# Decay attention and a mixture of experts: weights loaded a chunk later, ranks corrected by a small product, one fill instead of two, splits 6 pieces ahead

## The chip, the cores and the metric

The kernel runs on one core of one Trainium2 chip. The metric is the device time of one execution in microseconds, as the median of repeated runs. TensorE is called PE below, VectorE DVE, ScalarE ACT, GpSimd POOL, and SyncE SP; SP only issues transfers here.

## The reference, cut to what matters

Attention with a decay, in blocks, over 2 batches, 8 heads, 768 positions and head size 64; its output, as 1536 tokens of 512 numbers, goes into a mixture of 8 experts. Each token goes to the expert with the largest logit, at the next free place there; an expert takes at most 384 tokens.

```
intra = (qb @ kb.T * Dmask) @ vb
inter = (qb * lam_pow) @ kv_state
out[block] = intra + inter
kv_state = lam_block * kv_state + (kb * rev_pow).T @ vb
...
logits = x @ w_gate;  expert_idx = argmax(logits);  gate_w = softmax(logits)[expert_idx]
for i in range(N):                       # places in the order of the tokens
    e = expert_idx[i]
    if counts[e] < capacity: disp[e, counts[e]] = x[i]; counts[e] += 1
h = relu(disp @ w1);  y = h @ w2;  out[i] = gate_w[i] * y[expert_idx[i], pos[i]]
```

## The kernel before

The program is written out in one order by hand; each engine runs its own instructions in that order, and waits where data or a buffer is missing. It has three stages.

**Attention, 12 chunks of 128 positions** (the loop `for s in range(NTILE)`; two batches of 6 chunks). Step `s` places chunk `s-2`, multiplies chunk `s` with its masked scores (`attend`, line 442, and 450 for the part from the state), adds to the state (`state`, line 476, then `stt` on DVE, line 484), turns the output of chunk `s-1` into rows of tokens and logits (`turn`, lines 493 and 495), and makes the scores of chunk `s+2` (`score`, line 422). `choose` finds the expert of each token on DVE and ends with the one-hot rows `oh` (line 516). `place` multiplies `oh` with a triangle of ones and the running counts `cum` with ones, so that `rank` is the token's row in the DRAM table `xs`; `scatter` writes the rows there by an indirect transfer from POOL. POOL also makes `kd` and `qd`, the decayed keys and queries of later chunks.

**Weights.** They come as 64 pieces of 512 KB, 8 for each expert. `load_w` issues a piece on SP into one of 4 buffers `wraw`; `split_hi` on ACT makes its rounded part `whi`, and `split_lo` on DVE the rest `wlo` (line 113). The tables LOAD, HI and LO say in which step of the attention a piece is loaded and split: before, piece 0 is loaded in step 1, split on ACT in step 3 and on DVE in step 4. Since ACT and DVE take their work in order, a piece that is late holds what stands behind its split.

**Expert 0 early, then 7 experts.** Expert 0 gets its first 128 tokens from the first 7 chunks (EARLY) as the class `Solo`: `up`, `cross` (a transpose of the hidden rows), `down`; `first` runs between the end of the attention and the others, `second` holds a second 128 tokens. `shift()`, in step 8, counts the tokens of expert 0 in the first 7 chunks (a product into `early`, line 554) and adds what is missing to 128 into the running counts (line 559), so that later tokens of expert 0 begin at row 128. After the last chunk `count()` counts all tokens and makes `padi`, the row numbers of unused places, to which `pad` writes zeros by indirect transfers; `fill()` writes zeros over the whole place of FILLED experts at the start, and these need no `pad`. `load_rows(e)` reads an expert's rows back; it is on SP, so weight loads issued after it wait behind it. For the experts 1 to 7, `shuffle` and `trans` turn the rows (DVE, ACT, DVE), then come four products `h` (lines 778 and 782), each with `hf`, `hh`, `hl` on ACT and DVE, then four products `y` (line 810). After each of these eight, `next_w(j)` splits piece `j + 10` and loads piece `j + 14`.

Of the kernel before, what the change touches and what calls it, by code (L numbers as in the profile page):

```python
# [10 lines left out]
F16 = mybir.dt.float16  # L11
# [24 lines left out]
FILLED = 2  # L36
XO = 188
LOAD = {1: (0,), 2: (1,), 3: (2,), 4: (3, 4), **{s: (s,) for s in range(5, 12)}}
HI = {s: s - 3 for s in range(3, 12)}
LO = {s: s - 4 for s in range(4, 12)}  # L40
# [3 lines left out]
def kernel(  # L44
# [44 lines left out]
    padi = const.tile([P, E, 2], I32, name="padi")  # L89

# [10 lines left out]
    def split_hi(i):  # L101
        if i >= E * NWP:
            return
        hi = wsp_p.tile([P, WP], F32R, tag="whi", name="whi")
        nc.scalar.activation(out=hi, in_=raw[i], func=AF.Copy)  # L105
        wsp[i] = (hi, None)
# [144 lines left out]
    def attention():  # L251
        with ExitStack() as c2:
# [70 lines left out]
            nc.gpsimd.memset(zero, 0.0)  # L323
# [21 lines left out]
            def fill():  # L345
                for e in range(FILLED):
                    nc.sync.dma_start(
                        out=xs[e * STR:e * STR + RS].rearrange("(t p) c -> p t c", p=P),
                        in_=zero[:, None, :].to_broadcast([P, 2, ROW]),
                    )  # L350

            def tokens():
                nc.gpsimd.tensor_scalar(
                    out=base8, in0=iota_i, scalar1=float(STR), scalar2=None, op0=ALU.mult
                )
                nc.gpsimd.iota(padi, pattern=[[STR, E], [P, 2]], base=0, channel_multiplier=1)
                nc.gpsimd.tensor_copy(row, padi)
                nc.gpsimd.iota(toki, pattern=[[P, NTILE]], base=0, channel_multiplier=1)
                nc.gpsimd.tensor_copy(tokf, toki)
                nc.gpsimd.tensor_scalar(  # L360
                    out=xg_all[:, :, DM + 1], in0=tokf, scalar1=-1.0,
                    scalar2=float(NT), op0=ALU.mult, op1=ALU.add,
                )
# [121 lines left out]

            def turn(s):

                if s < 0:
                    return
                t = ps_1.tile([P, 2 * DM], F32, tag="tp", name="tp")  # L490
                tp[s] = t[:, 0:KD * XO].rearrange("p (k c) -> p k c", c=XO)
                nr[s] = t[:, 2 * DM - E:2 * DM]
                nc.tensor.matmul(nr[s], lhsT=ones, rhs=num, start=True, stop=True)
                for k in range(KD):
                    nc.tensor.matmul(tp[s][:, k, 0:P + E], lhsT=xT[s][:, k], rhs=iw[:, k], start=True, stop=True)  # L495

# [39 lines left out]
            def place(s):  # L536
                if s < 0:
                    return
                nc.tensor.matmul(rank, lhsT=upper, rhs=oneh[s], start=True, stop=False)
                nc.tensor.matmul(rank, lhsT=ones, rhs=cum[s], start=False, stop=True)  # L540
# [10 lines left out]
            def shift():  # L551

                c = cum[EARLY]
                nc.tensor.matmul(early, lhsT=ones, rhs=c, start=True, stop=True)
                nc.vector.tensor_scalar(
                    out=short, in0=early[:, 0:1], scalar1=float(P), scalar2=-1.0, op0=ALU.min, op1=ALU.mult
                )
                nc.vector.tensor_scalar(out=short, in0=short, scalar1=float(P), scalar2=None, op0=ALU.add)
                nc.vector.tensor_tensor(out=c[0:1, 0:1], in0=c[0:1, 0:1], in1=short[0:1], op=ALU.add)
# [26 lines left out]
            for s in range(NTILE):  # L586
# [14 lines left out]
                if s == EARLY + 1:  # L601
                    shift()
# [3 lines left out]
                choose(s - 1)  # L606
                rows(s - 1)
# [10 lines left out]
                load(s + 6, 0)  # L618
                if s == EARLY + 1:
                    load_rows(0, 0)  # L620
# [20 lines left out]
            def count():  # L641
                nc.tensor.matmul(early, lhsT=ones, rhs=cum[NTILE], start=True, stop=True)
# [13 lines left out]
            first.up(2, (tail(2), None, None))  # L656
            load_rows(0, 1)
            load_rows(1)
            first.cross(0)
            first.up(3, (count, None, None))  # L660
            split_lo(8)
            split_hi(9)
            first.down(0)
            first.cross(1)
            load_w(12)
            split_lo(9)
            load_w(13)
# [3 lines left out]
    def ffn(first):  # L671
        with ExitStack() as c2:
# [33 lines left out]
            def next_w(j):  # L706
                split_w(j + 10)
                load_w(j + 14)
# [26 lines left out]
            second.up(0)  # L735
            split_lo(10)
            load_w(14)
            second.up(1)
            split_hi(11)
            split_lo(11)  # L740
            load_w(15)
            second.up(2)
            shuffle(1, 0)
            second.cross(0)
            trans(1, 0)
            split_hi(12)
            second.up(3)
            split_lo(12)
            load_w(16)
            shuffle(1, 1)  # L750
            second.down(0)
            second.cross(1)
            trans(1, 1)
            for i, p in ((13, 1), (14, 2), (15, 3)):
                split_w(i)
                load_w(i + 4)
                second.down(p)
            pad(3, 0)
            pad(3, 1)
            split_w(16)  # L760
            load_w(20)
            split_w(17)
            load_w(21)
# [274 lines left out]
```

## Time and profile before

| | us |
|---|---|
| median of 3 runs | 260.01 |
| fastest and slowest of them | 259.89, 261.07 |
| the profiled execution, its own time | 257.97 |
| its span, first to last instruction | 256.2 |
| PE busy in the span | 237.2 (93%) |
| DVE busy | 172.2 (67%) |
| ACT busy | 144.6 (56%) |
| POOL busy | 76.9 (30%) |

Busy time of PE is modelled from pipelined starts, so it does not say how near PE is to its peak. The profiled execution lies 2.0 us under the median of the runs; 1.8 us of its own time lie outside the span.

### The profile page before, as it was taken

The page shows a single profiled execution, that of the slowest core. Times are in us where ns is not written, and L with a number is a line of the kernel's source. Part 1 is how long each engine was busy: PE and PEld are TensorE (multiplying, and loading weights), DVE is VectorE, ACT ScalarE, POOL GpSimd, SP SyncE. Part 2 cuts the span into 40 slices and gives each one's busy share as a digit, 9 for nine tenths or more (in the row PEclk, how much of TensorE's full clock was granted, in tenths as well). Part 3 has the DMA queues.
Part 4 walks back from the last instruction along what each step waited for, and adds up shares of the span by engine and source line. Part 5 has one row for each costly group of instructions (what it writes and reads, how often), then busy time and mean ns, then how long its engine had stood idle before and what let it go on. Part 6 is the DMA issues. An engine that isn't in the chain of part 4 may idle for free.

```text
span 256.2 us, 4967 instructions
## 1 busy us (share of the span) xinstructions
PE 237.2 (93%) x1832; PEld 199.7 (78%) x1832; DVE 172.2 (67%) x323; ACT 144.6 (56%) x267; POOL 76.9 (30%) x100
## 2 busy tenths in 40 slices
PE   7897998769799988899999999999999999999991
PEld 3686887658698967777987797798798789779891
DVE  5654677897536587669677777966976896683400
ACT  2225556938643585666656756765685576653310
POOL 7565557657230711000700330070051021011031
PEclk9999999999999999999999999999999999999998
DMA  5999999985537767965859859786884989602011
GB/s 121 410 338 377 411 387 406 412 313 178 174 147 172 257 180 242 303 222 194 262 137 324 244 179 288 260 260 157 280 274 158 294 242 273 186 0 75 0 42 26
DMA packets 27246, 58.94 MB, mean 230 GB/s; under 512 B 6274, under 2 KB 13444, under 8 KB 27216
## 3 DMA queue, kind: packets, MB, share of 16 engines
q1 hardware_dynamic: 23296, 51.41, 63.0%
q0 software_dynamic: 3216, 7.14, 7.4%
q8 instruction: 16, 0.26, 0.5%
q14 instruction: 14, 0.11, 0.2%
q10 hardware_dynamic: 704, 0.02, 0.2%
HBM read 50.37 MB, written 11.22 MB: 240 GB/s over the span
## 4 chain that ended last, share of the span: by engine, by line
issue 32%; PE 26%; DMA 15%; DVE 11%; ACT 6%; POOL 5%; SPq 2%; POOLq 1%; DVEq 0%; ACTq 0%
PE y L810 9%; DMA qk<-in_qkv 8%; PE h L778 7%; DMA wraw<-in_wp 6%; DVE wlo L113 4%; PE h L782 3%; ACT whi L105 3%; POOL xs L132 2%; PE tp L495 2%; POOL out L181 2%; PE x L442 2%; DMA xs<-zero,padi 2%; DVE hf L788 1%; PE sc L422 1%; ACT hh L791 1%
## 5 line engine op out<-in xcount | busy, mean ns | idle before, releaser
L113 DVE TENSOR_TENSOR wlo<-wraw,whi 128x1024 fp32r<-128x1024 f32 x64 | 78.2, 1233 | 14.0 <-ACT whi L105 12.6
L778 PE MATMUL h<-xhl,whi 128*128 128x464 f32 x224 | 73.6, 381 | 2.1 <-DVE hf L788 1.3
L105 ACT ACTIVATE whi<-wraw 128x1024 fp32r<-128x1024 f32 x64 | 66.0, 1046 | 14.2 <-DMA wraw<-in_wp 14.2
L782 PE MATMUL h<-xhl,wlo 128*128 128x232 f32 x224 | 60.2, 269 | 0.0
L181 POOL DMA_INDIRECT out<-y,ti x13 | 15.3, 1179 | 117.8 <-ACT y L819 116.0
L778 PEld LDWEIGHTS h<-xhl,whi 128*128 128x128 f32 x224 | 42.0, 188 | 9.1 <-DVE hf L788 1.9
L782 PEld LDWEIGHTS h<-xhl,wlo 128*128 128x128 f32 x224 | 42.7, 190 | 0.3
L810 PE MATMUL y<-whi,hh 128*128 128x512 f32 (+1 forms) x104 | 41.1, 396 | 0.0
L810 PE MATMUL y<-whi,hl 128*128 128x512 f32 (+1 forms) x104 | 41.1, 395 | 0.0
L810 PE MATMUL y<-wlo,hh 128*128 128x512 f32 (+1 forms) x104 | 40.9, 393 | 0.0
L791 ACT ACTIVATE hh<-hf 128x464 fp32r<-128x464 f32 x28 | 16.6, 592 | 32.4 <-DVE hf L788 32.4
L792 DVE SCALAR_TENSOR_TENSOR hl<-hf,hh 128x464 fp32r<-128x464 f32 x28 | 18.0, 643 | 18.4 <-ACT hh L791 18.4
L788 DVE TENSOR_TENSOR hf<-h,hf 128x464 f32<-128x464 f32 x28 | 17.8, 636 | 8.0 <-ACT hf L787 8.0
L810 PEld LDWEIGHTS y<-whi,hl 128*128 128x128 f32 (+1 forms) x104 | 18.6, 179 | 5.7
L810 PEld LDWEIGHTS y<-wlo,hh 128*128 128x128 f32 (+1 forms) x104 | 18.6, 179 | 5.4
L810 PEld LDWEIGHTS y<-whi,hh 128*128 128x128 f32 (+1 forms) x104 | 18.6, 178 | 5.3
L430 DVE TENSOR_TENSOR pt<-sc,dt 128x512 f32<-128x512 f32 x24 | 16.2, 687 | 4.1 <-PE sc L422 3.8
L787 ACT ACTIVATE hf<-h 128x464 f32<-128x464 f32 x28 | 15.3, 545 | 5.9 <-PE h L782 5.9
L565 POOL DMA_INDIRECT xs<-xg,slot x12 | 12.3, 1025 | 20.7 <-ACT slot L564 16.5
L422 PE MATMUL sc<-qk 64*128 64x128 f32 x192 | 14.2, 285 | 2.6 <-DMA qk<-in_qkv 2.6
L422 PEld LDWEIGHTS sc<-qk 64*128 64x128 f32 x192 | 11.9, 187 | 4.5 <-DMA qk<-in_qkv 2.7
L500 ACT ACTIVATE xg<-tp 128x512 f32<-128x512 f32 x12 | 7.1, 590 | 13.3 <-DVE oh L516 13.3
(127 smaller groups left out, 339.6 us busy)
## 6 DMA issues: line engine op xcount, KB each, us to landing
wraw<-in_wp SPq DMA_DIRECT2D x64, 512.0 KB, 5.0
qk<-in_qkv SPq DMA_DIRECT2D x12, 512.0 KB, 10.9
kv<-in_qkv SPq DMA_DIRECT2D x12, 512.0 KB, 11.2
rw<-xs SPq DMA_DIRECT2D x28, 128.0 KB, 3.1
xs<-zero SPq DMA_DIRECT2D x2, 514.0 KB, 10.8
rw<-xs SPq DMA_DIRECT2D x2, 257.0 KB, 3.7
out<-y,ti POOLq DMA_INDIRECT x13, 6.1
xs<-xg,slot POOLq DMA_INDIRECT x12, 5.2
```

The lines of the kernel that those rows point to most:

```text
L105: nc.scalar.activation(out=hi, in_=raw[i], func=AF.Copy)
L113: nc.vector.tensor_tensor(out=lo, in0=t, in1=hi.bitcast(F32), op=ALU.subtract)
L181: i = nc.gpsimd.indirect_dma_start(out=out, out_offset=bass.IndirectOffsetOnAxis(ap=ti[e][0:m, t:t + 1], axis=0), in_=y[0:m], in_offset=No ...
L422: nc.tensor.matmul(sc[s][r][:, a], lhsT=kT[rs, a], rhs=qT[rs, a], start=True, stop=True)
L430: nc.vector.tensor_tensor(out=pt[s][:, r], in0=sc[s][r], in1=dt[:, r], op=ALU.mult)
L778: nc.tensor.matmul(ps[:, f, 0:2 * SLOT], lhsT=wh[:, k, fs], rhs=x2[:, k], start=(k == 0), stop=False, skip_group_check=True,)
L782: nc.tensor.matmul(ps[:, f, 0:SLOT], lhsT=wl[:, k, fs], rhs=x2[:, k, 0], start=False, stop=(k == KD - 1), skip_group_check=True,)
L787: nc.scalar.activation(out=hf, in_=ps[:, :, SLOT:2 * SLOT], func=AF.Copy)
L788: nc.vector.tensor_tensor(out=hf, in0=ps[:, :, 0:SLOT], in1=hf, op=ALU.add)
L791: nc.scalar.activation(out=hh, in_=hf, func=AF.Relu)
L792: nc.vector.scalar_tensor_tensor(out=hl, in0=hf, scalar=0.0, in1=hh.bitcast(F32), op0=ALU.max, op1=ALU.subtract)
L810: nc.tensor.matmul(yp[t][0:m], lhsT=a[:, f, tsl], rhs=b[:, f], start=(p == 0 and f == 0 and n == 0), stop=(p == 3 and f == 1 and n == 2),)
```

## The change

It has six parts.

1. LOAD, HI and LO stand one step later for the first pieces: piece 0 is loaded in step 2, split on ACT in step 4, on DVE in step 5; pieces 9 and 10 are loaded together in step 11. Before step 12 eleven pieces are loaded instead of twelve, eight split on ACT instead of nine, seven on DVE instead of eight.
2. `shift()` no longer writes into `cum`. Its count is a product into the PSUM tile `tp` of the same step (issued in `turn(7)`), it stands after `choose(7)`, and it writes the missing number into a small tile `more`; `place` of chunk 7 and later, and `count`, add a product of ones and `more`.
3. FILLED is 1. The fill reads two adjoining zeroed rows of `xg` for each partition and writes them as one piece of 4112 bytes; before, 2056 bytes. Expert 1 gets two `pad` transfers after `count` instead, and `load_rows(1)` stands behind them.
4. `count` stands inside `up(2)` of the first half, before it was inside `up(3)`.
5. Splits run 6 pieces ahead of their use (AHEAD) instead of 10.
6. The order of the splits, of `cross`, and of `shuffle` and `trans` for expert 1 in the second half of expert 0 is rearranged.

```
-FILLED = 2
+FILLED = 1
+AHEAD = 6
-LOAD = {1: (0,), 2: (1,), 3: (2,), 4: (3, 4), **{s: (s,) for s in range(5, 12)}}
-HI = {s: s - 3 for s in range(3, 12)}
-LO = {s: s - 4 for s in range(4, 12)}
+LOAD = {2: (0,), 3: (1,), 4: (2,), 5: (3,), **{s: (s - 2,) for s in range(6, 12)}, 11: (9, 10)}
+HI = {s: s - 4 for s in range(4, 12)}
+LO = {s: s - 5 for s in range(5, 12)}
...
-                        out=xs[e * STR:e * STR + RS].rearrange("(t p) c -> p t c", p=P),
-                        in_=zero[:, None, :].to_broadcast([P, 2, ROW]),
+                        out=xs[e * STR:e * STR + RS].rearrange("(p t) c -> p (t c)", t=2),
+                        in_=xg_all[:, NTILE - 2:NTILE].rearrange("p t c -> p (t c)"),
...
+                if s == EARLY:
+                    c = t[:, 2 * DM - 2 * E:2 * DM - E]
+                    sofar.append(c[:, 0:1])
+                    nc.tensor.matmul(c, lhsT=ones, rhs=cum[EARLY], start=True, stop=True)
...
-                nc.tensor.matmul(rank, lhsT=ones, rhs=cum[s], start=False, stop=True)
+                nc.tensor.matmul(rank, lhsT=ones, rhs=cum[s], start=False, stop=(s < EARLY))
+                if s >= EARLY:
+                    nc.tensor.matmul(rank, lhsT=ones, rhs=more, start=False, stop=True)
...
-                c = cum[EARLY]
-                nc.tensor.matmul(early, lhsT=ones, rhs=c, start=True, stop=True)
                 nc.vector.tensor_scalar(
-                    out=short, in0=early[:, 0:1], scalar1=float(P), scalar2=-1.0, op0=ALU.min, op1=ALU.mult
+                    out=short, in0=sofar[0], scalar1=float(P), scalar2=-1.0, op0=ALU.min, op1=ALU.mult
+                )
+                nc.vector.tensor_scalar(
+                    out=more[0:1, 0:1], in0=short[0:1], scalar1=float(P), scalar2=None, op0=ALU.add
                 )
                 nc.vector.tensor_scalar(out=short, in0=short, scalar1=float(P), scalar2=None, op0=ALU.add)
-                nc.vector.tensor_tensor(out=c[0:1, 0:1], in0=c[0:1, 0:1], in1=short[0:1], op=ALU.add)
...
-            first.up(2, (tail(2), None, None))
+            first.up(2, (tail(2), count, None))
             load_rows(0, 1)
+            pad(1, 0)
+            pad(1, 1)
             load_rows(1)
+            split_lo(7)
             first.cross(0)
-            first.up(3, (count, None, None))
+            split_hi(8)
+            first.up(3)
             split_lo(8)
-            split_hi(9)
+            load_w(11)
...
-                split_w(j + 10)
-                load_w(j + 14)
+                split_w(j + AHEAD)
+                load_w(j + AHEAD + 4)
...
             second.up(1)
-            split_hi(11)
-            split_lo(11)
-            load_w(15)
             second.up(2)
-            shuffle(1, 0)
             second.cross(0)
-            trans(1, 0)
-            split_hi(12)
+            split_w(11)
+            load_w(15)
             second.up(3)
-            split_lo(12)
-            load_w(16)
-            shuffle(1, 1)
             second.down(0)
             second.cross(1)
+            shuffle(1, 0)
+            trans(1, 0)
+            shuffle(1, 1)
             trans(1, 1)
```

The first place is SP's list in the steps 0 to 3 of the attention: `xs` is the fill, `qk` and `kv` are the two halves of a chunk, `wraw` is a piece of weights. Before:

```order
L347 DMA xs<-zero 128x2x514 x2
L268 DMA kv<-in_qkv 128x1024
L268 DMA qk<-in_qkv 128x1024 x3
L268 DMA kv<-in_qkv 128x1024
L98 DMA wraw<-in_wp 128x1024
L268 DMA qk<-in_qkv 128x1024
L268 DMA kv<-in_qkv 128x1024
L98 DMA wraw<-in_wp 128x1024
```

And now, in the changed kernel, whose lines are numbered anew:

```order
L349 DMA xs<-xg 128x1028
L270 DMA kv<-in_qkv 128x1024
L270 DMA qk<-in_qkv 128x1024 x3
L270 DMA kv<-in_qkv 128x1024
L270 DMA qk<-in_qkv 128x1024
L270 DMA kv<-in_qkv 128x1024
L100 DMA wraw<-in_wp 128x1024
```

One fill is gone, and the first piece of weights stands behind two more halves of chunks.

The second place is DVE's list in step 8 of the attention, from the count of expert 0's tokens on (`short`, then `cum` or `more`) to the masks `pt` of step 9. Before:

```order
L555 TENSOR_SCALAR short<-st 128x1
L558 TENSOR_SCALAR short<-short 128x1
L559 TENSOR_TENSOR cum<-cum,short 1x1
L508 TENSOR_REDUCE l<-tp 128x8
L513 MAX m_920<-l 128x8
L514 MAX_INDEX i_79<-m_920,l 128x8
L516 TENSOR_TENSOR oh<-tp,i_79 128x8
L430 TENSOR_TENSOR pt<-sc,dt 128x512
```

And now:

```order
L529 TENSOR_TENSOR oh<-tp,i_79 128x8
L568 TENSOR_SCALAR short<-tp 128x1
L571 TENSOR_SCALAR more<-short 1x1
L574 TENSOR_SCALAR short<-short 128x1
L437 TENSOR_TENSOR pt<-sc,dt 128x512
L561 SCALAR_TENSOR_TENSOR pr,sraw<-st,oh 128x8
```

The three small instructions now stand behind `oh`; the one that wrote into `cum` is gone.

The third place is DVE's list at the end of expert 0, from the preparation of expert 1 (`ti`, `gt`, `xf`, `xhl`) to the first `hf` of expert 1; `solo_hl` belongs to the second half of expert 0. Before:

```order
L170 TENSOR_SCALAR ti<-wt 128x2
L174 TENSOR_SCALAR gt<-wt 128x2
L177 RECIPROCAL gt<-gt 128x2
L691 STREAM_TRANSPOSE xf<-rw 128x512
L230 TENSOR_TENSOR solo_hl<-solo_ps,solo_hh 128x512
L702 TENSOR_TENSOR xhl<-xf,xhl 128x2x232
L113 TENSOR_TENSOR wlo<-wraw,whi 128x1024
L691 STREAM_TRANSPOSE xf<-rw 128x512
L230 TENSOR_TENSOR solo_hl<-solo_ps,solo_hh 128x512
L702 TENSOR_TENSOR xhl<-xf,xhl 128x2x232
L113 TENSOR_TENSOR wlo<-wraw,whi 128x1024 x5
L788 TENSOR_TENSOR hf<-h,hf 128x464
```

And now:

```order
L232 TENSOR_TENSOR solo_hl<-solo_ps,solo_hh 128x512
L172 TENSOR_SCALAR ti<-wt 128x2
L176 TENSOR_SCALAR gt<-wt 128x2
L179 RECIPROCAL gt<-gt 128x2
L713 STREAM_TRANSPOSE xf<-rw 128x512
L724 TENSOR_TENSOR xhl<-xf,xhl 128x2x232
L713 STREAM_TRANSPOSE xf<-rw 128x512
L724 TENSOR_TENSOR xhl<-xf,xhl 128x2x232
L115 TENSOR_TENSOR wlo<-wraw,whi 128x1024 x2
L806 TENSOR_TENSOR hf<-h,hf 128x464
```

Both halves of the preparation now stand behind the last `solo_hl`, and two pieces are split between them and the first `hf` instead of five.

## Rows read from the trace of the kernel before

**Rows 1.** The page: TensorE's granted clock in 40 slices, tenths of full speed.

```profile
PEclk9999999999999999999999999999999999999998
```

**Rows 2.** Windows: stretch and length, busy PE, PEld, DVE, ACT, POOL, clock, DMA share, GB/s.

```profile
13.64:64.87 51.23, 44.58 (x708) 38.17 (x708) 36.40 (x107) 29.94 (x92) 31.33 (x36) 1.00 0.94 349
64.87:96.50 31.63, 29.74 (x222) 26.19 (x221) 18.86 (x48) 18.94 (x37) 9.14 (x11) 1.00 0.61 183
96.50:119.82 23.32, 21.98 (x113) 18.10 (x112) 18.12 (x24) 14.13 (x21) 1.25 (x1) 1.00 0.81 248
```

**Rows 3.** Timeline, PE: start, length, line, tiles, idle before and its releaser.

```profile
23.24 1.16 PE L422 MATMUL sc<-qk 64*128 64x128 f32 x16 [1.54 <-DMA qk<-in_qkv]
...
40.16 0.17 PE L493 MATMUL tp<-num,warm 128*128 128x8 f16 x1 [0.74 <-ACT xg L500]
47.78 0.17 PE L539 MATMUL st<-oh,upper 128*128 128x8 f16 x1 [0.48 <-DVE oh L516]
47.90 1.09 PE L442 MATMUL x<-pt,kv 128*64 128x128 f32 x16
51.61 0.18 PE L554 MATMUL st<-cum,warm 128*128 128x8 f16 x1 [1.40 <-DVE stt L484]
55.61 0.17 PE L539 MATMUL st<-oh,upper 128*128 128x8 f16 x1 [1.67 <-DVE oh L516]
55.73 1.09 PE L442 MATMUL x<-pt,kv 128*64 128x128 f32 x16
60.34 1.09 PE L442 MATMUL x<-pt,kv 128*64 128x128 f32 x16
```

**Rows 4.** Windows around the fill, columns as in group 2.

```profile
13.00:16.00 3.00, 3.00 (x62) 2.47 (x58) 1.39 (x3) 0.60 (x1) 3.00 (x4) 1.00 1.03 399
16.00:20.00 4.00, 4.00 (x63) 3.38 (x64) 2.56 (x10) 1.87 (x8) 1.26 (x2) 1.00 1.09 265
```

**Rows 5.** The page's groups: ACT's splits, and the idle time before them.

```profile
L105 ACT ACTIVATE whi<-wraw 128x1024 fp32r<-128x1024 f32 x64 | 66.0, 1046 | 14.2 <-DMA wraw<-in_wp 14.2
```

**Rows 6.** Timeline, DVE and POOL, in step 8.

```profile
48.85 1.27 POOL L397 TENSOR_TENSOR qd<-qk,qp 128x512 f32<-128x512 f32 x1
48.93 2.29 DVE L113 TENSOR_TENSOR wlo<-wraw,whi 128x1024 fp32r<-128x1024 f32 x1
...
51.82 0.16 DVE L555 TENSOR_SCALAR short<-st 128x1 f32<-128x1 f32 x1 [0.27 <-PE st L554]
...
52.27 2.50 DVE L559 TENSOR_TENSOR cum<-cum,short 1x1 f16<-1x1 f16 x1
...
53.49 1.26 POOL L397 TENSOR_TENSOR qd<-qk,qp 128x512 f32<-128x512 f32 x1
```

**Rows 7.** Timeline, PE, at the end of expert 0 and in expert 1.

```profile
90.41 0.50 PE L241 MATMUL solo_ps<-whi,solo_hl 128*128 128x512 f32 x1 [0.77 <-DVE solo_hl L230]
91.89 0.66 PE L227 MATMUL solo_ps<-ident,solo_raw 128*128 128x128 f32 x4 [0.26 <-ACT solo_raw L222]
...
102.59 0.48 PE L778 MATMUL h<-xhl,whi 128*128 128x464 f32 x1 [0.79 <-DVE hf L788]
...
105.98 0.48 PE L778 MATMUL h<-xhl,whi 128*128 128x464 f32 x1 [0.55 <-DVE hf L788]
```

**Rows 8.** The chain that ended last: start, length, work; two runs of `y`.

```profile
174.78 11.18 PE y L810 x48
...
196.37 11.18 PE y L810 x48
```

**Rows 9.** Groups by line: preparation of expert 1 to 7, and `solo_hl`.

```profile
L691 DVE STREAM_TRANSPOSE xf<-rw 128x512 f32<-128x512 f32 x14 | 9.9, 709 | 0.4 <-issue 0.4
L702 DVE TENSOR_TENSOR xhl<-xf,xhl 128x464 fp32r<-128x464 f32 x14 | 8.9, 634 | 0.1
```

**Rows 10.** DMA issues (us to landing), and SP's waits (total, times, longest).

```profile
xs<-zero,padi POOLq DMA_INDIRECT x12, 4.0
...
SPq L150 <- DMA xs<-zero,padi: 26.6, 4, 7.3
```

More of the change, by code (lines that the diff above doesn't have):

```diff
@@ L89 @@
     padi = const.tile([P, E, 2], I32, name="padi")
+    more = const.tile([P, E], F16, name="more")
     raw = {}
@@ L321, in powers @@
                     )
-            nc.gpsimd.memset(zero, 0.0)
+            nc.gpsimd.memset(xg_all[:, NTILE - 2:NTILE], 0.0)
             iota_i = ac.tile([P, E], U32, name="iota_i")
@@ L357, in tokens, with number @@
                 nc.gpsimd.tensor_copy(row, padi)
+                nc.gpsimd.memset(more, 0.0)
                 nc.gpsimd.iota(toki, pattern=[[P, NTILE]], base=0, channel_multiplier=1)
                 nc.gpsimd.tensor_copy(tokf, toki)
+                nc.gpsimd.memset(zero, 0.0)
+                number(slice(0, NTILE - 2))
+            def number(c):
                 nc.gpsimd.tensor_scalar(
-                    out=xg_all[:, :, DM + 1], in0=tokf, scalar1=-1.0,
+                    out=xg_all[:, c, DM + 1], in0=tokf[:, c], scalar1=-1.0,
                     scalar2=float(NT), op0=ALU.mult, op1=ALU.add,
@@ L484, in state @@
                     nc.vector.tensor_tensor(out=stt[s + 1], in0=tmp[s], in1=st, op=ALU.add)
+            sofar = []
             def turn(s):
@@ L600, in attention @@
                     state(s)
-                if s == EARLY + 1:
-                    shift()
                 if s in HI:
@@ L606, in attention @@
                 choose(s - 1)
+                if s == EARLY + 1:
+                    shift()
                 rows(s - 1)
@@ L618, in attention @@
                 load(s + 6, 0)
+                if s == EARLY - 1:
+                    number(slice(NTILE - 2, NTILE))
                 if s == EARLY + 1:
@@ L641, in count @@
             def count():
-                nc.tensor.matmul(early, lhsT=ones, rhs=cum[NTILE], start=True, stop=True)
+                nc.tensor.matmul(early, lhsT=ones, rhs=cum[NTILE], start=True, stop=False)
+                nc.tensor.matmul(early, lhsT=ones, rhs=more, start=False, stop=True)
                 nc.vector.tensor_copy(cnt8, early)
@@ L655, in attention @@
             first.up(1, (tail(0), None, None))
[L656 removed]
+            first.up(2, (tail(2), count, None))
             load_rows(0, 1)
+            pad(1, 0)
+            pad(1, 1)
             load_rows(1)
+            split_lo(7)
             first.cross(0)
[L660 removed]
+            split_hi(8)
+            first.up(3)
             split_lo(8)
[L662 removed]
+            load_w(11)
             first.down(0)
             first.cross(1)
+            split_hi(9)
+            split_lo(9)
             load_w(12)
[L666 to L667 removed]
             first.down(1)
@@ L735, in ffn @@
             second.up(0)
+            load_w(13)
             split_lo(10)
@@ L738, in ffn @@
             second.up(1)
-            split_hi(11)
-            split_lo(11)
+            second.up(2)
+            second.cross(0)
+            split_w(11)
             load_w(15)
-            second.up(2)
-            shuffle(1, 0)
-            second.cross(0)
-            trans(1, 0)
-            split_hi(12)
             second.up(3)
-            split_lo(12)
-            load_w(16)
-            shuffle(1, 1)
             second.down(0)
             second.cross(1)
+            shuffle(1, 0)
+            trans(1, 0)
+            shuffle(1, 1)
             trans(1, 1)
[L754 to L757, printed above, removed]
+            split_w(12)
+            load_w(16)
+            second.down(1)
+            second.down(2)
             pad(3, 0)
             pad(3, 1)
[L760 to L763, printed above, removed]
+            second.down(3)
+            split_w(13)
+            load_w(17)
             second.finish()
```

## The prediction

> **What bounds the kernel now.** I read the windows of the three stages first, then PE's timeline for the waits in each, then what was late there. The granted clock is at its upper level, 2.4 GHz, up to the last slice [rows 1], so no term below is a change of clock. PE is the engine whose waits end last, but not in the same way everywhere.
>
> - The attention from chunk 1 to chunk 11 takes 51.23 us, PE is busy for 44.58 of them, and the transfers run at 0.94 of the DMA engines' share, 349 GB/s [rows 2]. The reader should see that each of PE's long waits there has another releaser [rows 3]: 1.54 us for `qk` of chunk 4 (a transfer), 0.74 for `xg` and 0.48 for `oh` (ACT and DVE late), 1.40 and 1.67 around `shift` in step 8. An undisturbed step, from one `attend` to the next, takes 60.34 - 55.73 = 4.61 us; step 8 takes 55.73 - 47.90 = 7.83.
> - From chunk 11 to expert 1 PE is busy for 29.74 of 31.63 us; it waits 0.77 and 0.26 us in the second half of expert 0 [rows 2, 7].
> - Expert 1 takes 23.32 us [rows 2]. A later one takes 196.37 - 174.78 = 21.59 from its first `y` to the next one's [rows 8]. In expert 1 PE waits 0.79 and 0.55 us for `hf` on DVE [rows 7].
>
> Behind that the experts run with PE busy all but for small gaps, and the change leaves their products alone. What there is to gain or lose lies in the first 120 us.
>
> **The change, part by part.** Everything is summed as PE's time, against the profiled execution's own 257.97 us, and then set on the median of the runs, 260.01, 2.04 higher.
>
> *Fill and the first weights.* Two fills are 1.03 MB. While they were written, the rate fell from 399 to 265 GB/s for 4 us [rows 4], so they took 1.03 MB / 399 GB/s = 2.6 us of the transfers' time and 4 x (399 - 265) / 399 = 1.3 us more by the fall, 3.9 in all. One fill of the same kind costs half, 1.95; without the fall 1.3. So `qk` of chunk 4, which is behind it in SP's list, comes 1.95 to 2.6 us earlier, and PE's wait of 1.54 is covered by either: **-1.5**. The bound from below is -1.0, if the long packets fall further.
>
> *ACT's waits for weights.* ACT sat 14.2 us before splits, all of it for `wraw` [rows 5]; in the attention that made `xg` and `oh` late, 0.74 + 0.48 us on PE [rows 3]. Now the same transfers lie behind one fill less, and piece 0 is issued one step later but split one step later too, so the distance from issue to split stays two steps, 9.2 us. What shortens is the queue in front: 1.95 to 2.6 us of fill and the 1.3 us of piece 0 itself. I take **-1.2**; bounds 0 and -1.4.
>
> *`shift`.* Before, the product into `early` shares a PSUM tile with the state and waits for `stt`, which is behind a `wlo` of 2.29 us; then `oh` waits behind a `cum` of 2.50 us [rows 3, 6]. Now the product goes into `tp` and follows `turn`, and `oh` stands ahead of the three small instructions. They take 0.16 us each by the row of `short`, 0.5 us in all, before the `more` that `place(7)` wants and the masks of step 9: step 8 falls from 7.83 to 4.61 + 0.5 = 5.1, **-2.7**. The bounds come from `more`: it has no row. The nearest is `short`, also one tensor with a constant, 0.16; the other end is `cum`, 2.50, which with two SBUF inputs waited while POOL ran `kd` and `qd` up to 54.75 [rows 6]. I take the first, because `more` reads one tensor. The ends are -3.2 and -0.4.
> The Trainium skill ("SBUF — State Buffer", Who interferes with whom) says that a VectorE instruction with two SBUF inputs and a GpSimd instruction that reads SBUF block each other whole; the rows of `wlo` and `cum` agree with it, at 2.29 and 2.50 us. It adds that `tensor_scalar` can contend too, when it gets into a two-port mode, which no row here shows; by that the term would be -0.4 and the sum -4.3, by the row of `short` it is -2.7 and -6.6.
>
> *The products with `more`.* Five in `place`, one in `count`. The two products of `place` lie 0.12 us in front of `attend` (55.61 to 55.73) [rows 3], so one more is 0.06, and six make **+0.3**.
>
> *End of expert 0.* `wlo` of pieces 10 and 11 no longer stands in front of `solo_hl`; the waits of 0.77 and 0.26 go: **-1.0**; bounds 0 and -1.2, with a slow first product behind each wait. Piece 11 now comes behind `load_rows(1)`, and that behind two `pad` transfers (POOL about 2.2 us, landing 4.0 [rows 10]); ACT's split of it stands in front of the `raw` for `cross(1)`. By the order it fits with less than 1 us to spare.
>
> *Entry of expert 1.* The preparation stands as a whole behind the last `solo_hl`. From `cross(1)` on, DVE and ACT have in a row: transposes 0.4, `hh` 0.6, `hl` 0.7, three small 0.5, and twice `xf` 0.71, `xhl` on ACT 0.59, `xhl` on DVE 0.63 [rows 9], 6.1 us, with the hand-overs (0.05 each) 6.4. PE has in the same time transposes, 18 products `y` at 11.18 / 48 = 0.23 [rows 8], and the four first products `h` (0.65), 5.2. New wait: **+1.2**; bounds 0, if the hand-overs overlap, and +2.0, if they take twice as long. Against that the two waits in expert 1 go, since two pieces instead of five are split in front of its first `hf`: 23.32 - 21.59 = **-1.7**.
>
> *Splits 6 ahead.* A piece is still loaded four splits ahead, so `load_rows` holds SP's list as it did; six pieces are some 15 us of PE's time. I cost it at nothing; its cover is that distance, and where `load_rows(e + 2)` waits for `pad` (7.3 us at most [rows 10]) that is still enough. The gaps at the entries of experts 3 and 4, which come from that wait, stay. POOL's longer clearing at the start lies ahead of transfers that last longer: nothing.
>
> Sum: -1.5 - 1.2 - 2.7 + 0.3 - 1.0 + 1.2 - 1.7 = -6.6, so 251.4 on the profiled execution's scale and **253.4 us** on the runs' scale.
>
> **The rivals.**
>
> 1. *DVE and POOL hold each other.* `wlo` no longer waits for ACT and starts right behind the masks, where POOL may be in `qd`. The row for it is 2.29 instead of 1.23 us [rows 6]. If all seven `wlo` of the attention wait so, DVE gets 1.06 us more in each of seven steps. It is busy for 36.40 us in the ten steps [rows 2], 3.6 of 4.61 in a step, and the gaps between its small instructions come on top; I count 0.65 of the 1.06 as lost, 7 x 0.65 = 4.6 us: 258.0. Against it: in the undisturbed step at 55.73 nothing of it is seen. Chance 0.08.
> The rule of the Trainium skill named above ("SBUF — State Buffer", Who interferes with whom) would do just this, as each `wlo` has two SBUF inputs and `kd` and `qd` read SBUF.
> 2. *`more` waits as `cum` did.* Term by term -0.4 instead of -2.7: 255.7. Chance 0.13.
> 3. *Weights stay late.* If the queue in front does not shorten, ACT goes on waiting, in more steps than before since all pieces now have two steps only: the -1.2 goes, and four more waits of 0.5 come: 256.6. For it: the share of 0.94 [rows 2]. Against: less is transferred in front of it. Chance 0.12.
> 4. *Slower: expert 1's rows behind `pad`.* Everything on SP behind `load_rows(1)`, piece 11 first, then waits for two transfers that were not there. If they land late, ACT waits for piece 11, `raw` behind it, PE at `cross(1)`. With the longest wait seen, 7.3 instead of 4.0, 2.5 us are lost: 255.9. It decides the sign only when `pad` lands some 8 us later than 4.0, and then gives 261.5. Chance of that 0.03.
> 5. *Nothing comes of it*, since the transfers bound the attention whatever is waited for: then the bytes count, one fill and one piece less, 3.2 us, and the other gains up to chunk 11 go: with the end, 255.3 or, if the end gives nothing, 256.8. Inside the range; chance 0.06.
>
> **How the numbers follow.** The forecast has 0.58. Its own range adds the small bounds: 251.0 to 255.0. The range for 8 in 10 reaches to rivals 2 to 4 above, and below to all bounds of gain together (1.6 + 1.4 + 3.2 + 1.2 + 1.7 = 9.1, less 0.3: 251.2, with 0.8 for the two small gaps of the experts 3 and 4): 250.4 to 257.0. A measurement of this kernel can tell about 0.5% from no change, 1.3 us. Faster by more than that takes all cases but the worst of rivals 1 and 4 and part of 5: 0.92; within it 0.05; slower 0.03.
>
> **What would show it.** PE: no wait for `qk` near 23 us; step 8 near 5.1 us; chunk 11's `attend` some 5.1 us (1.5 + 1.2 + 2.7 - 0.3) earlier than 64.87; one wait of about 1.2 us for `xhl` at the entry of expert 1, and none for `hf` in it. DVE: `more` at 0.16, `wlo` at 1.23. ACT: less than 14.2 us for `wraw`. It would be wrong if `more` or many `wlo` take 2 us, if ACT waits for weights in each step, or if PE waits at `cross(1)` or for pieces in the experts, which would show that six pieces are too few.

## The result, and the profile after

The changed kernel takes 251.56 us (median of 4 runs, 250.66 to 252.51) against 259.95 (4 runs, 257.51 to 261.07) for the kernel before: a ratio of 0.969, 95% interval 0.961 to 0.977. The forecast was 253.4 with a range of 250.4 to 257.0. The profiled executions lie closer together, 252.51 against 257.97 us; the other 3 us between the medians are taken up further down.

Windows of the changed kernel, columns as in [rows 2], for the same three stretches (attend of chunk 1 to that of chunk 11, to expert 1, expert 1):

```profile
13.73:59.50 45.77, 44.62 (x712) 37.98 (x711) 35.01 (x106) 29.36 (x91) 36.70 (x38) 1.00 0.95 357
59.50:90.19 30.69, 29.31 (x225) 26.18 (x223) 16.50 (x45) 15.66 (x33) 12.80 (x13) 1.00 0.65 207
90.19:112.85 22.66, 21.72 (x113) 18.11 (x113) 17.57 (x25) 14.68 (x21) 1.44 (x1) 1.00 0.66 190
```

Against [rows 2] the stretches are 5.46, 0.94 and 0.66 us shorter. PE is busy for as long as before in the first one (44.62 and 44.58), so what went is waiting. The share of the transfers did not fall, 0.95 after 0.94, and the kernel still lost 5.5 us there.

PE's timeline of the changed kernel, the places that answer to [rows 3] and [rows 7]:

```profile
44.92 1.09 PE L449 MATMUL x<-pt,kv 128*64 128x128 f32 x16
...
48.70 0.17 PE L508 MATMUL tp<-cum,warm 128*128 128x8 f16 x1 [0.32 <-POOL cum L537]
...
50.23 1.09 PE L449 MATMUL x<-pt,kv 128*64 128x128 f32 x16
...
54.72 0.17 PE L552 MATMUL st<-oh,upper 128*128 128x8 f16 x1
54.75 0.17 PE L553 MATMUL st<-cum,warm 128*128 128x8 f16 x1
54.77 0.17 PE L555 MATMUL st<-more,warm 128*128 128x8 f16 x1
...
76.17 0.63 PE L200 MATMUL solo_ps<-ident,rw 128*128 128x128 f32 x4 [0.61 <-DMA rw<-xs]
...
91.93 0.47 PE L796 MATMUL h<-xhl,whi 128*128 128x464 f32 x1 [0.94 <-DVE xhl L724]
```

Step 8 is 50.23 - 44.92 = 5.31 us instead of 7.83. Both waits of [rows 3] around `shift` are gone; what stands there now is 0.32 us for `cum` on POOL. The waits for `qk`, `xg` and for `oh` at 47.78 do not come back, nor do the four of [rows 7]. New are 0.61 us for expert 0's second rows and 0.94 for `xhl` at the entry of expert 1.

DVE and POOL in steps 7 and 8 (answering to [rows 6]), from their two timelines of the changed kernel:

```profile
46.23 1.27 POOL L404 TENSOR_TENSOR qd<-qk,qp 128x512 f32<-128x512 f32 x1
47.46 1.18 POOL L537 TENSOR_TENSOR cum<-cum,oh 128x8 f16<-128x8 f16 x1
...
46.21 2.38 DVE L115 TENSOR_TENSOR wlo<-wraw,whi 128x1024 fp32r<-128x1024 f32 x1
...
49.76 0.15 DVE L568 TENSOR_SCALAR short<-tp 128x1 f32<-128x1 f32 x1
49.94 0.14 DVE L571 TENSOR_SCALAR more<-short 1x1 f16<-1x1 f32 x1
50.12 0.15 DVE L574 TENSOR_SCALAR short<-short 128x1 f32<-128x1 f32 x1
```

`more` takes 0.14 us, where the instruction that it replaces took 2.50 [rows 6]. But `wlo` takes 2.38 and ends 0.05 us before POOL's `cum` does. Five of the seven `wlo` of the attention take 1.5 to 2.4 us, where before only one did.

The end of the program is no part of the change. The last work of the chain, before and then after (start, length, what):

```profile
251.86 0.76 POOL out L850
```

```profile
245.03 0.76 POOL out L868
```

The spans end at 256.2 and 250.8 us, so 3.6 and 5.0 us behind the last scatter. In twelve further profiled executions this was 3.5 to 5.3. At the last scatter the two executions differ by 6.83 us, and the forecast's sum was 6.6.

### The profile page after: what moved, and what is told of

Its sections match the earlier page's. It is cut to its first block, busy times and chain, and to the rows that moved or that the text cites. A ratio compares the mean times of both kernels' runs of the same rounds, so it can differ in the third digit from the quotient of the medians.

```text
span 250.8 us, 4968 instructions
## 1 busy us (share of the span) xinstructions
PE 237.1 (95%) x1838; PEld 199.6 (80%) x1838; DVE 172.4 (69%) x323; ACT 144.5 (58%) x267; POOL 87.1 (35%) x105
## 4 chain that ended last, share of the span: by engine, by line
PE 45%; issue 15%; DVE 13%; DMA 11%; ACT 9%; POOL 2%; SPq 1%; POOLq 1%; DVEq 0%; ACTq 0%
PE y L828 13%; PE h L796 10%; DVE wlo L115 6%; DMA wraw<-in_wp 5%; PE h L800 5%; ACT whi L107 5%; PE tp L504 4%; PE sc L429 4%; PE x L449 3%; DMA qk<-in_qkv 3%; DVE hf L806 2%; PE x L457 2%; PE st L483 2%; DVE xhl L724 2%; PE solo_ps L219 1%
## 5 line engine op out<-in xcount | busy, mean ns | idle before, releaser
L115 DVE TENSOR_TENSOR wlo<-wraw,whi 128x1024 fp32r<-128x1024 f32 x64 | 80.9, 1273 | 12.0 <-ACT whi L107 10.1
L580 POOL DMA_INDIRECT xs<-xg,slot x12 | 14.2, 1180 | 11.1 <-ACT slot L579 7.3
L134 POOL DMA_INDIRECT xs<-zero,padi x14 | 16.1, 1146 | 4.3 <-issue 4.0
L723 ACT ACTIVATE xhl<-xf 128x464 fp32r<-128x464 f32 x14 | 8.3, 591 | 11.9 <-DVE xf L713 11.9
## 6 DMA issues: line engine op xcount, KB each, us to landing
rw<-xs SPq DMA_DIRECT2D x2, 257.0 KB
```

Source lines behind the costliest of these rows:

```text
L115: nc.vector.tensor_tensor(out=lo, in0=t, in1=hi.bitcast(F32), op=ALU.subtract)
L134: i = nc.gpsimd.indirect_dma_start(out=xs, out_offset=bass.IndirectOffsetOnAxis(ap=padi[:, e, t:t + 1], axis=0), in_=zero, in_offset=None, ...
```

## The experiments

Each kernel was run 4 to 12 times next to the kernel before. Ratios are to that kernel, with their 95% intervals. The last three columns are read from the profiled execution of each (us): when PE starts `attend` of chunks 4 and 11, the lengths of steps 7 and 8, and that of expert 1. The score of chunk 4 stands in step 2, so a wait for its `qk` is in the `attend` of chunk 4.

| kernel | median us | before us | ratio (interval) | `attend` 4, 11 | step 7, step 8 | expert 1 |
|---|---|---|---|---|---|---|
| kernel before, profiled | | | 1 | 29.08, 64.87 | 5.38, 7.83 | 23.32 |
| changed, first | 251.56 | 259.95 | 0.969 (0.961 to 0.977) | 27.56, 59.50 | 4.64, 5.31 | 22.66 |
| changed, again | 252.78 | 261.51 | 0.968 (0.963 to 0.973) | 27.52, 59.49 | 4.63, 5.34 | 22.66 |
| old shift in it | 256.83 | 261.51 | 0.984 (0.979 to 0.989) | 27.50, 63.21 | 5.92, 7.82 | 22.72 |
| old fills in it | 255.27 | 261.51 | 0.976 (0.971 to 0.980) | 32.38, 63.94 | 4.65, 4.93 | 22.66 |
| old weights in it | 251.84 | 261.51 | 0.966 (0.961 to 0.971) | 27.53, 60.10 | 4.91, 4.96 | 22.66 |
| two fills, big packets | 254.95 | 260.81 | 0.979 (0.974 to 0.984) | 30.03, 62.98 | 5.66, 4.98 | 22.67 |
| one fill, 2 KB packets | 252.46 | 260.81 | 0.968 (0.963 to 0.973) | 27.57, 60.49 | 5.97, 4.96 | 22.66 |
| ten ahead in it | 259.97 | 260.81 | 0.997 (0.994 to 1.000) | 27.57, 60.37 | 5.28, 4.98 | 30.30 |
| before + new shift | 257.18 | 260.81 | 0.986 (0.981 to 0.991) | 31.16, 64.06 | 5.96, 4.96 | 23.16 |
| before + six ahead | 259.33 | 261.12 | 0.993 (0.989 to 0.996) | 32.07, 67.38 | 5.44, 7.81 | 21.47 |
| changed + new entry | 251.84 | 261.12 | 0.964 (0.960 to 0.969) | 27.85, 61.09 | 6.30, 4.96 | 21.47 |
| changed + earlier loads | 251.66 | 261.12 | 0.965 (0.960 to 0.970) | 27.51, 59.45 | 4.63, 5.32 | 22.67 |
| changed + both | 251.06 | 261.74 | 0.961 (0.957 to 0.964) | 27.50, 59.42 | 4.64, 5.31 | 21.48 |

**The changed kernel again.**

> The changed kernel unaltered, as the mark for the three beside it. Theory of separate waits: 251.5 us or so, 8.4 below the kernel before (0.967), since the medians put the gain at 8.4 where the profiled executions differ by 5.5. If the profiled executions are nearer the truth it comes out at 5.5 to 6.5 below (0.975 to 0.979). The end of the program, from the last scatter on the GpSimd engine to the end of the span, took 3.6 us in the profiled run of before and 5.0 in that of the change: if that is a matter of the single execution, this run shows another value; if the change causes it, 5.0 again.

By the medians the gain is 8.7 us, so the larger figure of the first comparison repeats. The end behind the last scatter took 3.8 us this time: it belongs to the execution, not to the change.

**The old shift in the changed kernel.**

```
                 state(s)
+            if s == EARLY + 1:
+                shift()                    # with its product into early and the sum into cum
...
             choose(s - 1)
-            if s == EARLY + 1:
-                shift()
```

> The changed kernel with the old shift alone (product into early behind the state, correction written into cum, no products with more). Separate waits: the step from attend 8 to attend 9 goes back from 5.31 to some 7.8 us (the trace of before), less the six small products, so the time is 2.4 us above the changed kernel's, and entries of all experts move by the same 2.4. Rival, transfers bind the attention whatever is waited for: the step is longer but chunk 11's attend is not, and the time is within 0.5 us of the changed kernel's. Rival, half of it lies in the wlo that collides with GpSimd: with a wlo in step 8 that is now another piece at another place, 1.0 to 1.5 us.

PE's timeline in this run:

```profile
49.86 0.18 PE L562 MATMUL st<-cum,warm 128*128 128x8 f16 x1 [1.40 <-DVE stt L490]
53.86 0.17 PE L547 MATMUL st<-oh,upper 128*128 128x8 f16 x1 [1.67 <-DVE oh L524]
```

Both waits of [rows 3] come back with the same lengths, 1.40 and 1.67 us, and step 8 with 7.82. The medians put the old shift 4.1 us above the changed kernel, 3.7 at chunk 11. Of the latter 2.5 is step 8 and 1.28 step 7, whose instructions the edit leaves alone. The transfers as the only bound are out: chunk 11 moved.

**The new shift in the kernel before.** The same edit the other way round.

> The kernel before with the new shift alone (count into tp behind turn, correction in more, six products with it). Separate waits: step 8 falls from 7.83 to 5.1 us, chunk 11's attend from 64.87 to 62.3, time 2.4 below the kernel before. Taking the shift out of the changed kernel cost 4.0 by the medians and 3.7 at chunk 11 in the profile, of which 2.5 was step 8 and 1.3 step 7, where ACT waited 2.97 us for piece 2; if that 1.3 belongs to the shift, this run gains 3.7 to 4.0; if it is how late the weights land in one execution or another, 2.4. Rival, transfers bind: less than 1 us.

Step 8 falls to 4.96 us, 2.9 less. The median falls by 3.6, with an interval that reaches from 2.3 to 4.9. It holds the 2.5 to 2.9 of step 8, and does not exclude 4. What step 7 adds is seen in the table: it is 5.96 here with the new shift, and between 4.63 and 6.30 in the six executions that have the changed kernel's weights and one fill. So that 1.3 us is not the shift's.

**The old fills, two fills in big packets, one in small ones.**

```
-FILLED = 1
+FILLED = 2                       # old fills, and two in big packets
-  xs[...].rearrange("(p t) c -> p (t c)", t=2), in_=xg_all[...]
+  xs[...].rearrange("(t p) c -> p t c", p=P),   in_=zero[...]     # old fills, and one in small
-            pad(1, 0); pad(1, 1)              # where two are filled; count is back in up(3)
```

> The changed kernel with both static fills in 2 KB packets again, no pads for expert 1, the count at its old place. Separate waits: PE waits 1.5 us for qk of chunk 4 near 23 us again, and all attends behind it are 1.5 us later; at the end 0.8 us come back because the wait for rw near 76 us goes with the pads: net +0.7 to +1.5 us. Weights behind the fills come later too: up to 1.0 more through ACT's waits. Rival, the steps behind make good what the start loses: chunk 11's attend within 0.3 us of the changed kernel's, time the same.

> The changed kernel with two static fills, both in the big packets, no pads for expert 1, the count at its old place. If the packet is what counts, the rate falls hardly more than with one fill, the second costs its bytes, 0.53 MB at 400 GB/s, 1.3 us of the queue, and PE waits 0 to 1 us for qk of chunk 4; chunk 11's attend within 1 us of the changed kernel's 59.50, the time within 0.5 us of it, since the wait for rw near 76 us goes. If the number of fills counts, the run with both in 2 KB packets repeats itself: a wait of 3.3 us for qk, chunk 11's attend at 63.9, time +2.5.

> The changed kernel with its one static fill in 2 KB packets, pads for expert 1 kept. If the packet counts, half of the loss of the run with two such fills is here: a wait for qk of chunk 4 of 0.5 to 1.7 us, time +0.7 to +1.7. If the number of fills counts, no wait for qk and the time of the changed kernel within 0.3 us.

PE's timelines with two fills, in big packets, in small ones, and in small ones in the kernel before with the new shift:

```profile
24.19 1.16 PE L429 MATMUL sc<-qk 64*128 64x128 f32 x16 [2.39 <-DMA qk<-in_qkv]
```

```profile
25.05 1.71 PE L428 MATMUL sc<-qk 64*128 64x128 f32 x16 [3.22 <-DMA qk<-in_qkv]
```

```profile
23.83 1.61 PE L424 MATMUL sc<-qk 64*128 64x128 f32 x16 [1.78 <-DMA qk<-in_qkv]
```

What tells is the number of fills (and with it the bytes, 1.03 MB or half; no run tells these two apart), not the packet. With one fill PE has no wait for `qk` of chunk 4 in any of nine profiled executions, small packets among them. With two it waits 2.39 us with big packets and 1.54 to 3.22 with small ones. The medians are 2.5 us above that of a kernel with one fill run beside them, in both cases (254.95 against 252.46, 255.27 against 252.78). The expectation that big packets would make the second fill harmless failed.

**Six ahead in the kernel before.**

```
-                split_w(j + 10); load_w(j + 14)
+                split_w(j + 6);  load_w(j + 10)
-            for i, p in ((13, 1), (14, 2), (15, 3)): split_w(i); load_w(i + 4); second.down(p)
+            split_w(13); load_w(17); second.down(1 to 3)          # 16 and 17 left to next_w
```

> The kernel before with splits six ahead and nothing else: pieces 14 to 17 are no longer loaded and split between the end of expert 0 and the first hf of expert 1. Prediction's step: the two waits for hf in expert 1 (0.79 and 0.55 us) go, expert 1 falls from 23.32 to 21.6 to 22.0 us, time 1.3 to 1.7 below the kernel before. Rival, the distance of ten was paid for at later entries: as much more in waits for xhl or for pieces, time within 0.5 us. In the changed kernel the same edit undone cost 7.4 us, as the four pieces stood behind the whole preparation of expert 1; if six pieces are worth that by themselves, this run gains over 4 us. The attention of this run is that of before: its wait for qk of chunk 4 is a second look at the two fills. If the one of 1.54 us was short of what is usual, it is 2 to 3.5 us here and the profiled run is above 257.97 less the gain.

Expert 1 falls by 1.85 us and the median by 1.8 (interval 0.9 to 2.8), with no wait for `hf` and none for a piece. Its attention, which the edit leaves alone, is a second sample of the two fills. PE's timeline, and the windows (columns as in [rows 2]):

```profile
24.68 1.16 PE L422 MATMUL sc<-qk 64*128 64x128 f32 x16 [2.98 <-DMA qk<-in_qkv]
...
25.91 1.96 PE L442 MATMUL x<-pt,kv 128*64 128x128 f32 x16
```

```profile
18.00:20.00 2.00, 2.00 (x42) 1.52 (x40) 1.38 (x4) 1.87 (x8) 0.20 (x1) 1.00 1.39 243
20.00:22.00 2.00, 1.70 (x25) 1.43 (x25) 0.65 (x3) 0.74 (x3) 0.00 (x0) 1.00 0.69 150
22.00:24.00 2.00, 0.00 (x0) 0.00 (x0) 0.54 (x4) 1.26 (x6) 0.74 (x1) 1.00 0.99 404
...
26.00:28.00 2.00, 2.00 (x20) 1.67 (x24) 1.25 (x4) 0.20 (x1) 1.77 (x3) 0.50 1.04 414
28.00:30.00 2.00, 2.00 (x35) 1.60 (x32) 0.12 (x1) 0.60 (x1) 1.97 (x3) 0.66 1.01 410
```

The wait is 2.98 us where [rows 3] has 1.54: the rate fell to 150 GB/s. And behind it the granted clock is 0.50, its lower level of 1.2 GHz, for over 3 us; the sixteen products into `x` take 1.96 instead of 1.09 us. Steps 2 and 3 together take 32.07 - 18.25 = 13.82 us, where the profiled kernel before took 29.08 - 18.25 = 10.83 and the changed kernel 27.56 - 18.34 = 9.22. The profiled execution of the kernel before had a cheap pair of fills.

**Ten ahead in the changed kernel.**

```
-AHEAD = 6
+AHEAD = 10     # pieces 13 to 17 split and loaded behind trans(1, 1), in down(1) to down(3)
```

> The changed kernel with pieces split ten ahead again: four more pieces are loaded and split between the end of expert 0 and the first hf of expert 1. Prediction's step: the waits for hf in expert 1 return, 0.79 and 0.55 us in the trace of before, so expert 1 is 1.3 to 1.7 us longer than the changed kernel's 22.66, and all entries behind it are later by that. Rival, the ten pieces of distance pay it back at the entries behind (0.56 and 0.90 us of waits for xhl in the changed kernel): time within 0.5 us. Rival, the splits only fill idle time now that the preparation of expert 1 stands ahead of them: expert 1 as it is, 22.7 us.

PE, then ACT and DVE in their timelines:

```profile
103.43 0.76 PE L804 MATMUL h<-xhl,whi 128*128 128x464 f32 x1 [5.37 <-DVE hf L814]
...
92.45 3.89 ACT L107 ACTIVATE whi<-wraw 128x1024 fp32r<-128x1024 f32 x4
98.09 1.06 ACT L107 ACTIVATE whi<-wraw 128x1024 fp32r<-128x1024 f32 x1 [1.75 <-PE h L808]
100.51 1.06 ACT L107 ACTIVATE whi<-wraw 128x1024 fp32r<-128x1024 f32 x1 [1.36 <-DMA wraw<-in_wp]
101.47 0.67 ACT L250 ACTIVATE solo_y<-solo_ps,gt 128x512 f32<-128x512 f32 x1
102.04 0.55 ACT L813 ACTIVATE hf<-h 128x464 f32<-128x464 f32 x1
...
101.60 1.23 DVE L115 TENSOR_TENSOR wlo<-wraw,whi 128x1024 fp32r<-128x1024 f32 x1 [1.19 <-ACT whi L107]
...
102.74 0.63 DVE L814 TENSOR_TENSOR hf<-h,hf 128x464 f32<-128x464 f32 x1
```

Windows of the same stretch, columns as in [rows 2]:

```profile
98.00:103.00 5.00, 0.06 (x1) 0.00 (x0) 2.79 (x4) 3.14 (x4) 0.59 (x1) 0.79 0.96 345
103.00:105.00 2.00, 1.57 (x5) 1.47 (x6) 1.04 (x3) 1.59 (x3) 0.67 (x1) 0.50 0.72 246
105.00:107.00 2.00, 2.00 (x8) 1.77 (x8) 1.75 (x2) 0.60 (x2) 0.00 (x0) 0.50 0.95 309
```

None of the three theories foresaw this: expert 1 takes 7.6 us more, four times the price that the four pieces had in the old order. Six pieces stand as one block between the last `xhl` and the first `hf`; the fifth of them waits 1.75 us for PE's products `h`, the sixth 1.36 for its transfer, and `hf` comes behind both. Of the 7.6 us, 5.4 are the wait and the other 2.3 the clock: it fell while PE stood still and was 0.50 until after 107 us, with PE at work from 103.4. So this run does not price the edit by itself; the run before it does. It shows that the later preparation of expert 1 needs the shorter distance.

**The old weights in the changed kernel, and loads one step earlier.**

```
-LOAD = {2: (0,), 3: (1,), 4: (2,), 5: (3,), **{s: (s - 2,) ...}, 11: (9, 10)}
+LOAD = {1: (0,), 2: (1,), 3: (2,), 4: (3, 4), **{s: (s,) ...}}; HI, LO a step earlier   # old, and the splits in `first` as before
+LOAD = {s: (s - 1,) for s in range(1, 12)}                    # earlier loads, HI and LO as changed
```

> The changed kernel with the weights loaded and split a chunk earlier, as before, in the attention. Prediction's step: ACT waits for wraw some 3 to 5 us longer in the attention, xg and oh come late by 0.7 and 0.5 us in one or two steps, time +1.0 to +1.4 us. Rival, the fill alone had shortened the queue and a chunk later brings nothing: time within 0.3 us, ACT's wait for wraw in the attention under 3 us. Rival, the collisions of wlo with GpSimd are what matters (five wlo of over 1.5 us in the changed kernel, one before): wlo held by ACT start later and miss qd, fewer long wlo, time 0 to 1 us below.

> The changed kernel with each piece loaded one step earlier and split where it was, so three steps instead of two from load to split. If ACT's waits for wraw come from that distance, they fall from 2.9 us in the attention to under 1, step 7 is 4.6 us, chunk 11's attend at 59.5 or before, and the time is up to 1.3 below the changed kernel's, whose executions differ by whether step 7 has its 1.3 us. Rival, the transfers are what is full: a piece earlier pushes qk and kv behind it, waits for qk or kv appear in its place, and the time is the same or up to 1 us more.

The old weights bring nothing that can be told: 0.966 beside 0.968. Loads a step earlier take all of ACT's waits for pieces out of the attention. The split `whi` by tile from 20 to 66 us, what ACT waited for ahead of it (us, times), in the changed kernel with one small fill and then with the earlier loads:

```profile
L107 ACT ACTIVATE whi<-wraw x8: 1042/1054/1058, 31.5 to 62.7; 128x1024 fp32r<-128x1024 f32 x8
its engine sat idle before it (us, times) until:
  DMA wraw<-in_wp: 6.1, 3
```

```profile
L107 ACT ACTIVATE whi<-wraw x8: 1042/1044/1052, 30.0 to 61.7; 128x1024 fp32r<-128x1024 f32 x8
its engine sat idle before it (us, times) until:
who waited for it (us, times):
```

The one with the small fill waits most of the three with that attention; in the two profiles of the changed kernel itself the same wait is 2.9 and 2.3 us, in three waits. The time from issue to landing of the pieces says why there are such waits; 16 to 50 us, min/median/max in the kernel before:

```profile
DMA to landing us min/median/max: 10.3/11.6/12.0
```

Two steps are 9.2 us and too short for 11.6; three are 13.8. But the time to landing is not the same each time: piece 2 is issued at 30.3 us in the changed kernel and in the one with the small fill, and ACT, which waits for it in both, has it 8.7 us later in the one (38.95) and 11.5 in the other (41.79). With two steps, step 7 is 4.6 us in two executions and 5.3 to 6.3 in four; with three it was 4.63 and 4.64 in both (the second in the last run), which are only two. No `qk` or `kv` was late for it.

**Both transposes ahead of the splits.**

```
             shuffle(1, 0)
-            trans(1, 0)
             shuffle(1, 1)
+            trans(1, 0)
             trans(1, 1)
```

> The changed kernel with both transposes of expert 1 ahead of both splits of its rows: DVE has the second xf while ACT has the first xhl. If the wait of 1.1 us at the entry of expert 1 is the two hand-overs between DVE and ACT (0.66 us each before the two xhl), it goes or falls under 0.2, expert 1 falls from 22.66 to 21.6, time 1.0 below the changed kernel's 252.6. Rival, it only moves the wait behind the next hand-over (hf or the split of piece 12 and 13): time within 0.4.

DVE's timeline:

```profile
89.60 1.30 DVE L713 STREAM_TRANSPOSE xf<-rw 128x512 f32<-128x512 f32 x2
90.98 1.24 DVE L724 TENSOR_TENSOR xhl<-xf,xhl 128x464 fp32r<-128x464 f32 x2
```

DVE no longer waits for ACT between them, PE has no wait at the entry, and expert 1 takes 21.47 us, 1.19 less. The ratio is 0.964, beside 0.968 and 0.969 of the changed kernel: too near to tell. Step 7 took 1.7 us more in this execution than in the changed kernel's.

**Both additions.**

> The changed kernel with two additions together: both transposes of expert 1 ahead of its splits, and each piece loaded a step earlier. Each took its wait away by itself in the profile (1.1 us at the entry of expert 1; all of ACT's waits for wraw, and the 1.3 us of step 7 that come and go with them), though neither was told apart from the changed kernel by the medians (251.84 and 251.66 beside 251.6 to 252.8). If the two waits are separate, this run has neither: chunk 11's attend at 59.5, expert 1 in 21.5 us, entry of expert 2 at 111.7 instead of 112.8, time 250.3 to 251.3, ratio to the kernel before 0.958 to 0.962. Rival, what is saved early is lost at the entries of later experts, where rows land late in some executions (0.3 to 1.7 us): 251.7, as each alone.

Windows of this run, attend of chunk 1 to chunk 11, to expert 1, expert 1:

```profile
13.66:59.42 45.76, 44.84 (x712) 37.99 (x711) 34.99 (x106) 29.14 (x91) 36.77 (x38) 1.00 0.97 365
59.42:90.01 30.59, 29.27 (x225) 26.11 (x223) 17.09 (x46) 16.58 (x35) 12.79 (x13) 1.00 0.61 197
90.01:111.49 21.48, 21.48 (x114) 18.10 (x113) 16.93 (x24) 13.80 (x20) 1.44 (x1) 1.00 0.78 197
```

All three marks are as expected, PE is busy through the whole of expert 1, and the ratio of 0.961 (0.957 to 0.964) is the lowest of all the kernels. It lies 0.8% below that of the changed kernel; the intervals still touch, so that it is the faster of the two is not shown.

## Why the prediction was right, and where it was not

- **The bound.** That PE's waits end last, each with its own cause, and not the transfers: right. The transfers' share is 0.95 and the stretch 5.5 us shorter; shift, fills and six ahead each moved the time by themselves.
- **The fill, -1.5: the step that was mis-sized.** It took the wait of 1.54 us in one execution as the whole price and the bound at -1.6. Two fills cost 1.6, 2.5, 3.4, 4.6 and 4.8 us in the five profiled executions that have them, 3.4 in the mean (from the `attend` of chunk 2 to that of chunk 4, less 9.22), and 2.5 by the medians of the two kernels that have a second fill instead of the pads. The profiled execution of the kernel before is the cheapest of the five, and of the 60 other executions of that kernel only one is shorter than its 257.97 us (257.51, in the first comparison).
- **The clock, put at nothing.** That no term is a change of clock held for the execution that was read, whose mean granted clock is 0.997, and not for others: it is below 0.991 in 30 of the 56 executions of that kernel beside the experiments, and in none of the 40 of kernels with one fill, the new shift and six ahead. In the three profiled executions with two fills where it fell, that was 1.6 of their price. A second profile of the unaltered kernel before was not taken, so for its other executions this is worked out, not seen.
- **ACT's waits for weights, -1.2: wrong, and hidden by the execution.** The prediction kept the distance of two steps, 9.2 us, and let the queue in front get shorter. But a landing takes 11.6 us in the median, which the trace of before had shown, and two steps stay too short, by more or less in one execution or another. Of the 14.2 us of [rows 5] only 7.7 lay in the attention; they become 2.9 in the profiled pair, and 2.3 to 6.1 in the other five profiled executions with the new tables and one fill. Steps 6 and 7, where PE paid for them, take 10.05 us together in the profile of before and 8.75 in that of the change, so the pair shows -1.3. But the four profiled executions with the old tables have 9.85 in the mean (9.74 the one of them with one fill), the six with the new ones and one fill 9.67 (two of them 8.8, four 10.0 to 10.4): -0.2. That is rival 3 in its first half, the -1.2 that goes; its four more waits of 0.5 did not come.
- **The sum.** That -6.6 stands beside 6.83 in the profiled pair is luck in part: the one execution had cheap fills, the other no late piece in step 7, and the two errors have opposite signs. With -3.4 for the fill and -0.2 for ACT's waits it is -7.5, inside the intervals of both comparisons by the medians (8.4, from 6.1 to 10.1, and 8.7, from 7.0 to 9.6). The range held either way.
- **The shift, -2.7: right.** Step 8 is 5.31 us, or 4.96 where step 7 had its wait already; 5.1 was forecast. `more` takes 0.14, so rival 2 fell. The products with it cost 0.03 each (step 9 is 4.64 instead of 4.61).
- **The end of expert 0, -1.0, and the entry, +1.2: right.** The stretch is 0.94 us shorter, with a wait of 0.61 for rows in it that was not forecast (it is there, at 0.23 to 0.61, in all but one of the kernels with pads for expert 1, and in none with two fills instead). The new wait is 0.94 idle, 1.1 with the slow start behind it; reordering the transposes took it away, so it is the two hand-overs between DVE and ACT.
- **Six ahead: right, -1.7 and no cost.** By itself it gave -1.85 in expert 1.
- **Rival 1, DVE and POOL: its mechanism came, its price did not.** The Trainium skill ("SBUF — State Buffer", Who interferes with whom) says that VectorE with two SBUF inputs and GpSimd reading SBUF block each other for a whole instruction; the trace agrees, with `wlo` at 2.38 us beside `qd` and `cum`. The step of 0.65 us lost of each 1.06 was wrong: steps 9 and 10 are 4.64 and 4.63 us with a `wlo` of 1.76 in each. PE pays once, 0.32 us for `cum` in step 8.
- **Rival 4, rows behind `pad`: small where it came.** SP waits for `pad` 5 times, 31.9 us, instead of 4 times, 26.6 [rows 10], but in the changed kernel PE does not wait at `cross(1)`. With the earlier loads ACT waits 1.04 us for the piece in front of the `raw` for `cross(1)` and PE 0.46 at `cross(1)`; with ten ahead PE waits 0.67 there, where 2.5 had been forecast for the worst.
- **Rival 5** did not come: the shift moves no bytes, and taking it out moved the `attend` of chunk 11 by 3.7 us, 2.5 of them in step 8.

## What to carry to other kernels

Price a stall from more than one execution: the one that is profiled can be the cheap one, and a kernel that differs elsewhere gives a second sample for nothing. Compare the distance between a load and its use with the measured time to landing, not with what the queue in front saves, and over several executions. Before a preparation is moved behind other work, count what is then queued in one block ahead of the next instruction that PE needs: the same four splits cost 1.8 us in one order and 7.6 in another.

## What the hardware showed that was not expected

- A stall of PE can cost more than its length. Behind waits for `qk` of 1.78, 2.98 and 3.22 us the granted clock fell to 0.5 (1.2 GHz), and within the 5.37 us in expert 1 too; it stayed at 1.00 behind 1.54 and 2.39. Where it fell, 1.6 us came on top of the wait each time in the attention (steps 2 and 3 less 9.22 and less the wait; 0.07 where it did not fall) and 2.3 in expert 1.
- The same two fills of 1.03 MB let the rate fall to 265 GB/s over 4 us in one execution [rows 4] and to 150 over 2 us in another; with one fill PE waited for `qk` of chunk 4 in none of nine executions, in small or big packets.
- From the last scatter to the end of the span 3.5 to 5.3 us pass, by execution: 5.0 and 3.8 in two executions of one kernel.
